# Turning the third group of tokens by transposing transfers, in a fused FFT filter and token-shift MLP kernel

## Chip, core and metric

The kernel runs on one core of a Trainium2 chip. The metric is the device time of one execution in microseconds (us). The core has TensorE (PE, with a separate row PEld for its weight loads), VectorE (DVE), ScalarE (ACT), GpSimd (POOL) and SyncE (SP), whose queue issues every transfer of this kernel.

## The reference

One sequence `x` of 2048 tokens and 448 channels. With `xn` the layer norm of `x` over channels:

```
xn  = layernorm(x)
A   = irfft2(rfft2(xn) * (w_r + i w_i))          # over tokens and channels
h   = gelu(layernorm(xn) @ w1)                   # 448 x 448
hs  = [h0 down 1 | h1 up 1 | h2 down 2 | h3 up 2] @ w2   # quarters of h shifted along tokens
x1  = xn + hs
B   = x1 + gelu(layernorm(x1) @ w3) @ w4         # 448 x 1792, 1792 x 448
out = x + A + B
```

## The kernel before

**Tiles and groups.** The tokens lie in 16 blocks of 128 (token = 16 x partition + block), in four groups of four blocks: group 0 is blocks 14, 15, 0, 1, group 1 is 2 to 5, group 2 is 6 to 9, group 3 is 10 to 13 (`GRP`). A shift along tokens by 1 or 2 is a look at the neighbouring block, so `w2` of a block needs `h` of the blocks at distance 1 and 2.

**Two halves of every number.** Matmuls run in float16. Each operand is split into a high half (ACT rounds to float16) and a low half (DVE or POOL subtracts the high half), and each product is three passes: high by high, high by low, low by high. Weights are first scaled by a power of two that is found from the sum of their squares: ACT squares a piece and accumulates into a column of `m1` to `m4` (`squares`, L243), DVE adds the columns (`pt`, L248), PE adds over the partitions with a matrix of ones (`pm`, L254, in `powers`), DVE makes the scale from the exponent (`pe`, L257 to L260). For w3 this gives `s3`, then eight `w3_split` (ACT L287, DVE L288); for w4 `s4`, then seven `w4_split`.

**The stage around the change, some 10 to 100 us.** For each group:

- `norm1` normalizes the four blocks in place (`xt`).
- Channels are brought to the partitions as `xT`: seven slots of 128 rows, of which the first three and a half hold the high halves and the rest the low ones. Groups 0 to 2 do this with `turn_pe` and `turn_copy`: 16 PE transposes by the identity for a group (L403, tiles `pta`), ACT copies (L413) and DVE subtracts (L414) out of PSUM. Group 3 uses `turn(3)`: ACT and DVE split the normalized block first (L825 to L827), then four transposing transfers, one for a block, write `xT` directly (L828).
- `w1_unit` runs 11 matmuls for a block (L453, tiles `pw1_gi`), a gelu in place (L474), the split into `hs` or a part of `x2mem` (L475, L476), and a transposing transfer into `hT` (L479; called `h0` to `h3` by group, `h30` is group 3's first block).
- `w2_mm`/`w2_tile` runs 12 matmuls for a block (L497, tiles `pw2_b`), DVE adds the result to `xt` (L504).
- `ln2` normalizes blocks again (L525 to L538) and sends them by transposing transfers into `x2all` (L540; tiles `y0`, `y2` and so on).

Behind it comes the MLP by pairs of blocks G = 0 to 7: `front` (L424, tiles `pw3_Gf`, 22 matmuls of 256 columns, gelu L749, split L752 and L753) and `back` (L772). Between the pairs the kernel places the FFT's steps.

**Memory that is shared.** `w1s`, `w2s`, `x2`/`x3` (the split blocks of `turn`), `y` and others take turns in two staging tiles (`stage0`, `stage1`). `w4raw` lies in the same memory `x2mem` as `x2all` from its second quarter on. PSUM banks come in tags of two: `mm`, `tr`, `acc`, `sp`.

**Order.** A scheduler puts the instructions of each engine into one fixed order by its own model; `with behind(key)` says that what stands inside is placed after the instructions kept under that key. That is a placement and not a wait. Each engine then takes its list strictly in order, SP too, so a transfer whose data is not there holds up those behind it. A transposing transfer occupies SP's queue for over a microsecond.

The lines before that are moved:

```
    T1(2)                                   # L922: 16 PE transposes, ACT and DVE copies
    with behind("h", 1, 3):
        load_w3([3])                        # L924: the last 64 rows of w3, loaded twice,
                                            #   into both halves of the partitions (L218)
    for k in range(4):                      # L939: squares of the four tiles of w3
        with behind(*(("a2",), ("a2",), (2, 0), (2, 1))[k]):
            squares(m3[:, k:k + 1], w3raw[:, k])
    with behind("t", 3), behind("h", 2, 3), behind("b0"):
        for i in range(4):                  # L952: w4 in four transfers (L229)
            load_w4(i)
```

Of the kernel before, what the change touches and what calls it, by code (L numbers as in the profile page):

```python
# [13 lines left out]
F16 = mybir.dt.float16  # L14
I32 = mybir.dt.int32
AF = mybir.ActivationFunctionType
ALU = mybir.AluOpType
AX = mybir.AxisListType

S, D, DF, F = 2048, 448, 225, 1792  # L20
# [12 lines left out]
PACE = [(0, 6), (1, 1), (1, 2), (1, 4), (1, 5), (2, 0), (2, 1), (2, 3)]  # L33
FOLD = [(0, 5), (1, 0), (1, 1), (1, 3), (1, 4), (1, 6), (2, 0), (2, 2)]
PIN = [("a3",), ("a3",), ("a3",), ("a3",)]
WMAX = [(1, 4), (1, 5), (1, 6), (2, 0), (2, 1), (2, 2), (2, 3), (2, 4)]
LATE = [(2, 2), (2, 3), (2, 4), (2, 5)]
HS = 3
INV, LAG = 4, 2
# [82 lines left out]
def body(tc, nc, x, wf, w1, w2, w3, w4, c_g, c_n, c_small, out):  # L122
    V, A, P, T, SY = nc.vector, nc.scalar, nc.gpsimd, nc.tensor, nc.sync
# [28 lines left out]
    def bank(tag, name):  # L152
        return ps.tile([128, 512], F32, tag=tag, bufs=2, name=name)
# [17 lines left out]
    def stage(name, n, side, dtype=F32):  # L171
        t = pw.tile([128, 1808], F32, tag=f"stage{side}", bufs=1, name=name)
        return (t if dtype is F32 else t.bitcast(dtype))[:, :n]
# [13 lines left out]
    ones = pc.tile([128, 128], F32, name="ones")  # L187
# [24 lines left out]
    def load_w3(ts):  # L212
        for t in ts:
            if t < 3:
                SY.dma_start(w3raw[:, t], w3[128 * t:128 * t + 128])
            else:
                for h in range(2):
                    SY.dma_start(w3raw[64 * h:64 * h + 64, 3], w3[384:448])  # L218

    load_w3([0, 1])  # L220
    load_x(3)
    load_w3([2])
    x2mem = pw.tile([128, 9 * F], F16, name="x2mem")
    x2all = x2mem[:, 0:8 * F].rearrange("p (j t n) -> p j t n", j=4, t=7)
    w4raw = x2mem.bitcast(F32)[:, F:].rearrange("p (f n) -> p f n", f=14)
# [2 lines left out]
    def load_w4(i):  # L228
        SY.dma_start(w4raw[:, W4F[i]:W4F[i + 1]], w4[:, W4F[i]:W4F[i + 1]])  # L229
# [9 lines left out]
    def squares(col, src, junk=None):  # L239

        n = src.shape[-1]
        junk = xr.bitcast(F16) if junk is None else junk
        return A.activation(out=junk[:src.shape[0], :n], in_=src, func=AF.Square, scale=2.0 ** -20, accum_out=col)  # L243

    def powers(m, n, key, tag="acc", mid=None):

        t = pc.tile([128, 1], F32, name=f"pt{key}")
        i = V.tensor_reduce(out=t, in_=m[:, :n + 1], axis=AX.X, op=ALU.add)  # L248
        after["t" + key] = (i.ins,)
        if mid:  # L250
            with behind("t" + key):
                mid()
        pm = bank(tag, f"pm{key}") if isinstance(tag, str) else tag
        i = T.matmul(pm[:, 0:1], ones, t, start=True, stop=True)  # L254
        after["p" + key] = (i.ins,)
        e = pc.tile([128, 3], I32, name=f"pe{key}")
        V.tensor_scalar(out=e[:, 0:1], in0=pm.bitcast(I32)[:, 0:1], scalar1=1, scalar2=0x7F800000,  # L257
                        op0=ALU.logical_shift_right, op1=ALU.bitwise_and)
        V.tensor_scalar(out=e[:, 1:2], in0=e[:, 0:1], scalar1=-1, scalar2=185 << 23, op0=ALU.mult, op1=ALU.add)
        i = V.tensor_scalar(out=e[:, 2:3], in0=e[:, 0:1], scalar1=1, scalar2=69 << 23, op0=ALU.mult, op1=ALU.add)  # L260
        after["s" + key] = (i.ins,)
        return e.bitcast(F32)[:, 1:2], e.bitcast(F32)[:, 2:3]
# [127 lines left out]
    @contextlib.contextmanager  # L390
    def behind(*key):
        key = key if len(key) > 1 else key[0]
        with contextlib.ExitStack() as st:
            for i in after[key]:
                st.enter_context(tc.issue_after(i))
            yield
# [20 lines left out]
    def T1(g, ts=range(4)):  # L417
        for t in ts:
            turn_copy(g, t, turn_pe(g, t))
# [27 lines left out]
    def w1_in(g, units, ts, passes=range(3)):  # L447
        for p in passes:
            for t in ts:
                for i, pm in units:  # L450
                    wi, xi = ((0, 0), (0, 4), (4, 0))[p]
                    if t < 3 or p != 1:
                        m = T.matmul(pm[:, :D], xTs[g][:, xi + t, 128 * i:128 * i + 128], w1p[:, wi + t],  # L453
                                     start=t == 0 and p == 0, stop=t == 3 and p == 2)
        return m
# [8 lines left out]

    def w1_unit(g, i, pm=None):
        if pm is None:
            pm = bank(("tr" if g == 1 else "mm", "acc")[i // 2], f"pw1_{g}{i}")
            w1_in(g, [(i, pm)], range(4))
        c = CS[GRP[g][i]]
        pm = pm[:, :D]  # L470
        pv_ = pm.rearrange("p (k n) -> p k n", k=4)
        h = hs_buf[c % (HS if g == 3 else HS + 2)]
        with behind(0, i - 2) if g == 0 and i > 1 else contextlib.nullcontext():
            A.activation(out=pm, in_=pm, func=AF.Gelu_apprx_tanh, scale=gsc[:, c:c + 1])  # L474
        u = A.activation(out=h[:, 0, :, 0:112], in_=pv_, func=AF.Copy, scale=h1)  # L475
        v = V.scalar_tensor_tensor(out=h[:, 1, :, 0:112], in0=pv_, scalar=h1, in1=h[:, 0, :, 0:112],  # L476
                                   op0=ALU.mult, op1=ALU.subtract)
        o = h_at(g, i)
        d = SY.dma_start_transpose(out=hT[g][:, :, o:o + 128], in_=h.rearrange("p i k n -> p (i k n)"))  # L479
        after[g, i] = u.ins, v.ins  # L480
        after["h", g, i] = (d.ins,)
# [2 lines left out]

    def w2_mm(b, ks):
        if b not in w2b:
            w2b[b] = bank("sp", f"pw2_{b}")
        for k in ks:
            src, o = b - SHIFT[k], 1
            if src < 0:  # L490
                src, o = src + NB, 0
            elif src >= NB:
                src, o = src - NB, 2
            g, i = WHERE[src]
            o += h_at(g, i) - 1
            for hi, wi in ((0, 0), (0, 1), (1, 0)):
                m = T.matmul(w2b[b][:, :D], hT[g][:112, 4 * hi + k, o:o + 128], w2p[:, wi, k],  # L497
                             start=k == 2 and hi + wi == 0, stop=k == 3 and hi == 1)
        after["w2", b] = (m.ins,)

    def w2_tile(b, ks=(2, 0, 1, 3)):
        w2_mm(b, ks)
        pm = w2b.pop(b)
        V.scalar_tensor_tensor(out=xb(b), in0=xb(b), scalar=cs[:, CS[b]:CS[b] + 1], in1=pm[:, :D],  # L504
                               op0=ALU.mult, op1=ALU.add)
# [313 lines left out]
    def turn(g):  # L819

        xTs[g] = p1.tile([128, 7, 512], F16, tag="xT", bufs=2, name=f"xT{g}")
        y = stage(f"x{g}", 8 * D, 1, F16).rearrange("p (i n) -> p i n", i=4)
        for i, b in enumerate(GRP[g]):
            h, x_ = y[:, i], xb(b)
            u = A.activation(out=h[:, 0:D], in_=x_, func=AF.Copy)  # L825
            V.tensor_tensor(out=h[:, 448:512], in0=x_[:, 384:448], in1=h[:, 384:448], op=ALU.subtract)
            v = V.tensor_tensor(out=h[:, 512:896], in0=x_[:, 0:384], in1=h[:, 0:384], op=ALU.subtract)  # L827
            d = SY.dma_start_transpose(out=xTs[g][:, :, 128 * i:128 * i + 128], in_=h)  # L828
        after["t", g], after[f"a{g}"] = (d.ins,), (u.ins, v.ins)

    def w3_split(i):
        t, cl = i % 4, slice(896 * (i // 4), 896 * (i // 4) + 896)
# [81 lines left out]
            i = P.tensor_tensor(out=w2p[:, 1, k], in0=w2s[:112, k], in1=w2p[:, 0, k], op=ALU.subtract)  # L914
    after["w2p"] = (i.ins,)
    h_alloc(1)
    for k in range(4):
        w1_unit(1, k)
    for b in range(2):
        w2_mm(b, (2, 0))  # L920
    after["T", 2] = after["w2", 1]
    T1(2)  # L922
    with behind("h", 1, 3):
        load_w3([3])  # L924
    with behind("w2p"):
        n1[0][2]()
        n1[1][2]()
        for f in n1[2][:3]:
            f()
    for b in range(2):  # L930
        with behind("T", 2):
            w2_tile(b, (1, 3))
    with behind("a2"):
        n1 = [norm1(3, [P, P, P, P])]
# [1 line left out]
    with behind("w2", 1):  # L936
        for k in range(4):
            w1_unit(2, k)
    for k in range(4):  # L939
        with behind(*(("a2",), ("a2",), (2, 0), (2, 1))[k]):  # L940
            squares(m3[:, k:k + 1], w3raw[:, k])
    s3, r3 = powers(m3, 4, "3", "mm")
    h3 = pc.tile([128, 1], F32, name="h3")
    V.tensor_scalar(out=h3, in0=s3, scalar1=2.0 ** -5, scalar2=None, op0=ALU.mult)
    for b in range(2, 4):
        w2_tile(b)
    turn(3)
    for f in n1[0][:3]:
        f()
    ln2([0, 1], [A, P])  # L950
    with behind("t", 3), behind("h", 2, 3), behind("b0"):
        for i in range(4):  # L952
            load_w4(i)
    for b in range(4, 8):
        w2_tile(b)
        with behind(*PIN[b - 4]):
            w3_split(2 * b - 8)
            w3_split(2 * b - 7)
            for i in (2 * b - 10, 2 * b - 9):
                if i >= 0:  # L960
                    squares(m4[:, i:i + 1], flat(w4raw[:, 2 * i:2 * i + 2]), junk4)
    squares(m4[:, 6:7], flat(w4raw[:, 12:14]), junk4)
    ln2([2, 3], [A, P])
    h_alloc(3)
    for k in range(4):
        w1_unit(3, k)
    with behind("h", 3, 3):
        SY.dma_start(csm, c_small)
    s4, r4 = powers(m4, 7, "4")
    p34 = pc.tile([128, 2], F32, name="p34")  # L970
    V.scalar_tensor_tensor(out=p34[:, 1:2], in0=r3, scalar=2.0 ** 5, in1=r4, op0=ALU.mult, op1=ALU.mult)
# [104 lines left out]
```

## Time and profile before

| | |
|---|---|
| median of 3 runs | 413.37 us (413.05 to 413.66) |
| profiled execution | 413.19 us |
| its span in the profile | 411.4 us |
| mean granted TensorE clock | 0.999 |
| PE busy | 406.0 us, 99% of the span |
| DVE, ACT, POOL busy | 72%, 60%, 28% |
| q1, the queue of all transfers | 43.5% of 16 engines' span |

A row of a timeline is: start and length in us, engine, line, operation, output and inputs, count, and in brackets the idle time before it with what ended it. A row of the groups is: line, engine, operation, names, shapes, count, then busy us and mean ns of one, then idle time before. "DMA to landing" is the time from the start of a transfer's issue to its last byte's arrival. Lines L... are those of the kernel before. PE's matmul rows overlap by about 0.16 us, so the price of one in a row of many is the distance between starts.

### The profile page before, as it was taken

Reading aid. Unit: us, or ns where it says so; the run is one execution under the profiler, and the core shown is the slowest. Engines: PE = TensorE matmul, PEld = TensorE weight load, DVE = VectorE, ACT = ScalarE, POOL = GpSimd, SP = SyncE. Lnnn points to the kernel's source line nnn. Section 1 sums busy time; section 2 is a strip of 40 time slices with the busy share of each in tenths; the row PEclk is TensorE's granted clock in tenths of the full one; section 3 lists DMA queues with packets and bytes.
Section 4 is the critical chain, followed back from the end, with each engine's and each line's share of the span. In section 5 each row is a group of like instructions: output and inputs, shape, how many; then the busy total and the mean of one; then the engine's idle time right before and its main releaser. Section 6 shows DMA issues by size and latency. Waiting matters only on the chain.

```text
span 411.4 us, 8535 instructions
## 1 busy us (share of the span) xinstructions
PE 406.0 (99%) x3314; PEld 290.1 (71%) x3314; DVE 294.4 (72%) x638; ACT 247.7 (60%) x427; POOL 114.6 (28%) x205
## 2 busy tenths in 40 slices
PE   8999999999999999999999999999999999999996
PEld 3655555666667877776887888777776776677885
DVE  5988999897644758863689889875776787667122
ACT  4697979964638766862678888873343434342321
POOL 2987810011217746400031121211212221121000
PEclk9999999999999999999999999999999999999999
DMA  8979499806811383437056655610000213233001
GB/s 279 365 219 202 96 175 324 192 2 142 173 47 45 91 274 132 120 84 165 13 141 178 154 142 143 170 56 2 2 0 2 69 50 107 69 94 130 24 0 46
DMA packets 53496, 48.53 MB, mean 118 GB/s; under 512 B 37600, under 2 KB 48480, under 8 KB 53456
## 3 DMA queue, kind: packets, MB, share of 16 engines
q1 hardware_dynamic: 53456, 47.99, 43.5%
q8 instruction: 26, 0.43, 0.4%
q14 instruction: 14, 0.11, 0.1%
HBM read 35.52 MB, written 3.67 MB: 95 GB/s over the span
## 4 chain that ended last, share of the span: by engine, by line
PE 93%; DVE 3%; DMA 2%; ACT 1%; POOL 1%; issue 0%
PE pw L424 33%; PE acc L772 31%; PE pw L497 8%; PE pw L453 6%; PE pu L693 3%; PE ps L590 3%; PE pp L647 2%; PE pe L713 2%; PE px L664 2%; PE py L735 2%; DMA h<-x2mem 1%; DMA xt<-x 1%; DVE sta L312 1%; PE pta L403 1%; DVE xT L414 0%; DVE xt L352 0%
## 5 line engine op out<-in xcount | busy, mean ns | idle before, releaser
L424 PE MATMUL pw<-x2mem,w3p 128*128 128x256 f16 x1232 | 149.6, 273 | 0.0
L772 PE MATMUL acc<-w4p,hf 128*128 128x448 f16 (+1 forms) x714 | 138.0, 341 | 0.0
L424 PEld LDWEIGHTS <-w3p 128*128 128x128 f16 x1232 | 118.6, 98 | 19.4
L772 PEld LDWEIGHTS <-hf 128*128 128x128 f16 x714 | 69.4, 98 | 48.3 <-DVE hf L753 0.3
L749 ACT ACTIVATE pw<-pw,pe 128x512 f32<-128x512 f32 x56 | 36.7, 656 | 64.6 <-PE pw L424 63.4
L753 DVE SCALAR_TENSOR_TENSOR hf<-pw,h,hf 128x512 f16<-128x512 f32 x56 | 41.9, 749 | 43.6 <-ACT hf L752 43.3
L497 PE MATMUL pw<-w2p,h 112*128 112x448 f16 x192 | 39.4, 352 | 0.1
L752 ACT ACTIVATE hf<-pw,h 128x512 f16<-128x512 f32 x56 | 38.4, 685 | 1.2
L674 POOL TENSOR_TENSOR z<-te 128x450 f32<-128x450 f32 x16 | 16.0, 1003 | 73.0 <-DVE te L672 69.2
L453 PE MATMUL pw<-w1p,xT 128*128 128x448 f16 x176 | 35.1, 352 | 0.3 <-ACT xT L413 0.3
L720 POOL TENSOR_TENSOR e<-e 128x226 f32<-128x226 f32 x16 | 11.5, 721 | 77.8 <-ACT e L717 74.6
L497 PEld LDWEIGHTS <-h 112*128 112x128 f16 x192 | 18.6, 98 | 16.2 <-DMA h<-x2mem 0.5
L453 PEld LDWEIGHTS <-xT 128*128 128x128 f16 x176 | 17.1, 99 | 15.9 <-ACT xT L413 0.5
L654 ACT ACTIVATE pf<-pp 64x450 f16<-64x450 f32 x32 | 17.4, 543 | 16.7 <-DVE pf L655 8.3
L717 ACT ACTIVATE e<-pe 128x452 f32<-128x452 f32 x16 | 8.8, 548 | 26.4 <-PE pe L713 26.4
L655 DVE TENSOR_TENSOR pf<-pp,pf 64x450 f16<-64x450 f32 x32 | 19.9, 622 | 5.9 <-ACT pf L654 5.6
L570 POOL TENSOR_TENSOR xr<-xf 128x452 f32<-128x452 f32 x8 | 8.9, 1115 | 32.0 <-issue 27.6
L669 ACT ACTIVATE te<-px 64x450 f32<-64x450 f32 x32 | 17.3, 539 | 0.5
L728 DVE TENSOR_TENSOR vh<-e,vh 128x448 f16<-128x448 f32 x16 | 10.0, 625 | 9.7 <-ACT vh L727 9.7
L573 POOL TENSOR_TENSOR f<-xr 128x452 f32<-128x452 f32 x16 | 16.1, 1030 | 0.6
L581 DVE TENSOR_TENSOR xh<-f,xh 128x452 f16<-128x452 f32 x16 | 12.7, 833 | 5.0 <-ACT xh L580 5.0
L722 DVE TENSOR_TENSOR e<-e 128x113 f32<-128x113 f32 x16 | 9.9, 618 | 7.8 <-POOL e L720 7.8
(172 smaller groups left out, 600.5 us busy)
## 6 DMA issues: line engine op xcount, KB each, us to landing
wc<-wf SPq DMA_DIRECT2D x32, 225.0 KB, 3.6
wl<-wf SPq DMA_DIRECT2D x8, 450.0 KB, 3.7
xf<-x SPq DMA_DIRECT2D x8, 448.0 KB, 3.4
xt<-x SPq DMA_DIRECT2D x3, 896.0 KB, 11.1
w3raw<-w SPq DMA_DIRECT2D x3, 896.0 KB, 14.6
xr<-x SPq DMA_DIRECT2D x12, 224.0 KB, 2.6
out<-xr SPq DMA_DIRECT2D x12, 224.0 KB, 1.9
gn<-c_g SPq DMA_DIRECT2D x16, 128.0 KB, 3.2
```

The lines of the kernel that those rows point to most:

```text
L424: T.matmul(ps_out, wp[:, wi + t, cols], xT[:, xi + t, tok], start=t == 0 and wi + xi == 0, stop=t == 3 and wi == 4)
L453: m = T.matmul(pm[:, :D], xTs[g][:, xi + t, 128 * i:128 * i + 128], w1p[:, wi + t], start=t == 0 and p == 0, stop=t == 3 and p == 2)
L497: m = T.matmul(w2b[b][:, :D], hT[g][:112, 4 * hi + k, o:o + 128], w2p[:, wi, k], start=k == 2 and hi + wi == 0, stop=k == 3 and hi == 1)
L573: P.tensor_tensor(out=f[:, :, k:k + 2].rearrange("p b s d -> p s b d"), in0=u[:, :, 0], in1=u[:, :, 1], op=op)
L654: A.activation(out=hi, in_=src, func=AF.Copy)
L655: V.tensor_tensor(out=lo, in0=src, in1=hi, op=ALU.subtract)
L669: i = A.activation(out=e[64 * h:64 * h + 64], in_=px_[64 - 64 * h:128 - 64 * h, :2 * DF], func=AF.Copy)
L674: P.tensor_tensor(out=z, in0=t[:, 0], in1=t[:, 1], op=ALU.add)
L749: A.activation(out=pm, in_=pm, func=AF.Gelu_apprx_tanh, scale=r3)
L752: i = A.activation(out=h[:, 0], in_=pm, func=AF.Copy, scale=h3)
L753: j = V.scalar_tensor_tensor(out=h[:, 1], in0=pm, scalar=h3, in1=h[:, 0], op0=ALU.mult, op1=ALU.subtract)
L772: m = T.matmul(to, h[:, hi, o:o + 128], w4p[0][:, wi, f, r], start=f == 0 and n == 0, stop=f == 13 and n == 2)
```

## The change

- Group 2 is turned like group 3: `turn(2)`, four transposing transfers, called behind `w1_unit(1, 0)`, instead of `T1(2)`. Its split blocks lie in `stage0`. The splits of group 1's blocks 2 and 3 are placed behind those of group 2.
- In PE's order the place of the transposes is taken by the first matmuls of `pw2_2` and `pw2_3`, which now use banks of tag `mm`; `pw1_2k` uses `tr` instead of `mm`.
- w3's last 64 rows are loaded once, with the early loads, and copied on chip into the other half of the partitions behind `h20`. Their squares are taken over 64 rows only.
- The product for s3 stands behind `pw1_23`; the eight splits of w3 are placed behind h23's split.
- w4's first two transfers keep their place in the program; the last two, and all seven squares, are placed behind group 3's `h`.
- The maximum of the filter's third piece is placed one step later (`WMAX`).

```diff
-WMAX = [(1, 4), (1, 5), (1, 6), (2, 0), (2, 1), (2, 2), (2, 3), (2, 4)]
+WMAX = [(1, 4), (1, 5), (2, 0), (2, 0), (2, 1), (2, 2), (2, 3), (2, 4)]
...
-                for h in range(2):
-                    SY.dma_start(w3raw[64 * h:64 * h + 64, 3], w3[384:448])
+                SY.dma_start(w3raw[0:64, 3], w3[384:448])
...
-    load_w3([2])
+    load_w3([2, 3])
...
-    def powers(m, n, key, tag="acc", mid=None):
+    def powers(m, n, key, tag="acc", mid=None, pin=None):
...
-        i = T.matmul(pm[:, 0:1], ones, t, start=True, stop=True)
+        with behind(*pin) if pin else contextlib.nullcontext():
+            i = T.matmul(pm[:, 0:1], ones, t, start=True, stop=True)
...
     def w1_unit(g, i, pm=None):
         if pm is None:
-            pm = bank(("tr" if g == 1 else "mm", "acc")[i // 2], f"pw1_{g}{i}")
-            w1_in(g, [(i, pm)], range(4))
+            pm = bank(("tr" if g < 3 else "mm", "acc")[i // 2], f"pw1_{g}{i}")
+            after["u", g, i] = (w1_in(g, [(i, pm)], range(4)).ins,)
...
-        u = A.activation(out=h[:, 0, :, 0:112], in_=pv_, func=AF.Copy, scale=h1)
-        v = V.scalar_tensor_tensor(out=h[:, 1, :, 0:112], in0=pv_, scalar=h1, in1=h[:, 0, :, 0:112],
-                                   op0=ALU.mult, op1=ALU.subtract)
+        with behind("a2") if g == 1 and i > 1 else contextlib.nullcontext():
+            u = A.activation(out=h[:, 0, :, 0:112], in_=pv_, func=AF.Copy, scale=h1)
+            v = V.scalar_tensor_tensor(out=h[:, 1, :, 0:112], in0=pv_, scalar=h1, in1=h[:, 0, :, 0:112],
+                                       op0=ALU.mult, op1=ALU.subtract)
...
-            w2b[b] = bank("sp", f"pw2_{b}")
+            w2b[b] = bank("mm" if b in (2, 3) else "sp", f"pw2_{b}")
...
     def turn(g):
         xTs[g] = p1.tile([128, 7, 512], F16, tag="xT", bufs=2, name=f"xT{g}")
-        y = stage(f"x{g}", 8 * D, 1, F16).rearrange("p (i n) -> p i n", i=4)
+        y = stage(f"x{g}", 8 * D, g - 2, F16).rearrange("p (i n) -> p i n", i=4)
+        done = ()
         for i, b in enumerate(GRP[g]):
             h, x_ = y[:, i], xb(b)
             u = A.activation(out=h[:, 0:D], in_=x_, func=AF.Copy)
             V.tensor_tensor(out=h[:, 448:512], in0=x_[:, 384:448], in1=h[:, 384:448], op=ALU.subtract)
             v = V.tensor_tensor(out=h[:, 512:896], in0=x_[:, 0:384], in1=h[:, 0:384], op=ALU.subtract)
             d = SY.dma_start_transpose(out=xTs[g][:, :, 128 * i:128 * i + 128], in_=h)
-        after["t", g], after[f"a{g}"] = (d.ins,), (u.ins, v.ins)
+            done += (u.ins, v.ins)
+        after["t", g], after[f"a{g}"] = (d.ins,), done
...
     h_alloc(1)
-    for k in range(4):
+    w1_unit(1, 0)
+    turn(2)
+    for k in range(1, 4):
         w1_unit(1, k)
-    for b in range(2):
-        w2_mm(b, (2, 0))
-    after["T", 2] = after["w2", 1]
-    T1(2)
-    with behind("h", 1, 3):
-        load_w3([3])
+    for b, ks in ((0, (2, 0)), (1, (2, 0)), (2, (2, 0)), (3, (2,))):
+        w2_mm(b, ks)
...
-    for b in range(2):
-        with behind("T", 2):
+    with behind("w2", 3):
+        for b in range(2):
             w2_tile(b, (1, 3))
...
+    with behind("h", 2, 0):
+        SY.dma_start(w3raw[64:128, 3], w3raw[0:64, 3])
     for k in range(4):
-        with behind(*(("a2",), ("a2",), (2, 0), (2, 1))[k]):
-            squares(m3[:, k:k + 1], w3raw[:, k])
-    s3, r3 = powers(m3, 4, "3", "mm")
+        n = 128 if k < 3 else 64
+        with behind(*((1, 3), (1, 3), (1, 3), (2, 0))[k]):
+            squares(m3[:n, k:k + 1], w3raw[:n, k])
+    s3, r3 = powers(m3, 4, "3", "sp", pin=("u", 2, 3))
...
-    for b in range(2, 4):
-        w2_tile(b)
+    with behind("p3"):
+        w2_tile(2, (1, 3))
+    w2_tile(3, (0, 1, 3))
     turn(3)
...
     with behind("t", 3), behind("h", 2, 3), behind("b0"):
-        for i in range(4):
+        for i in range(2):
             load_w4(i)
     for b in range(4, 8):
         w2_tile(b)
-        with behind(*PIN[b - 4]):
+        with behind(*PIN[b - 4]), behind(2, 3):
             w3_split(2 * b - 8)
             w3_split(2 * b - 7)
-            for i in (2 * b - 10, 2 * b - 9):
-                if i >= 0:
-                    squares(m4[:, i:i + 1], flat(w4raw[:, 2 * i:2 * i + 2]), junk4)
-    squares(m4[:, 6:7], flat(w4raw[:, 12:14]), junk4)
     ln2([2, 3], [A, P])
     h_alloc(3)
     for k in range(4):
         w1_unit(3, k)
     with behind("h", 3, 3):
+        for i in range(2, 4):
+            load_w4(i)
         SY.dma_start(csm, c_small)
+    for i in range(7):
+        with behind(3, 3):
+            squares(m4[:, i:i + 1], flat(w4raw[:, 2 * i:2 * i + 2]), junk4)
```

## The prediction

> **What bounds the kernel now.** I read the page first. TensorE (PE) is busy for the whole span, and the chain that ended last runs through it:
>
> ```profile
> span 411.4 us, 8535 instructions
> PE 406.0 (99%) x3314; PEld 290.1 (71%) x3314; DVE 294.4 (72%) x638; ACT 247.7 (60%) x427; POOL 114.6 (28%) x205
> ...
> PE 93%; DVE 3%; DMA 2%; ACT 1%; POOL 1%; issue 0%
> ```
>
> The second view was PE's waits. It lists three, together 2 us, all before 12 us, so from there on time is saved by taking work off PE, and lost by any new wait of PE:
>
> ```profile
> PE wps L808 <- DVE wsrc L186: 1.2, 1, 1.2
> PE wps L846 <- DVE xt L352: 0.5, 1, 0.5
> PE pw L453 <- ACT xT L413: 0.3, 1, 0.3
> ```
>
> Third, PE's timeline through the stage that the change rebuilds, 30 to 100 us (start, length, line):
>
> ```profile
> 30.74 2.44 PE L497 MATMUL pw<-w2p,h 112*128 112x448 f16 x12
> 33.01 1.91 PE L403 MATMUL pta<-ident,xt 128*128 128x128 f32 x16
> 34.76 2.68 PE L497 MATMUL pw<-w2p,h 112*128 112x448 f16 x12
> 37.28 8.49 PE L453 MATMUL pw<-w1p,xT 128*128 128x448 f16 x44
> 45.61 6.98 PE L497 MATMUL pw<-w2p,h 112*128 112x448 f16 x36
> 52.42 0.28 PE L254 MATMUL pm<-pt,ones 128*128 128x1 f32 x2
> ...
> 100.19 2.57 PE L424 MATMUL pw<-x2mem,w3p 128*128 128x256 f16 x22
> 102.59 2.43 PE L772 MATMUL acc<-w4p,hf 128*128 128x448 f16 x12
> ```
>
> Rows overlap, so a price is the distance between starts: the 16 transposes of group 2 take 34.76 - 33.01 = 1.75 us; a 448-column matmul (52.42 - 45.61)/36 = 0.189 us; a 256-column one (102.59 - 100.19)/22 = 0.109 us; a `pm` product 0.14 us.
>
> **The change part by part.** *Removed from PE:* the 16 transposes, -1.75 us. In the built order PE is otherwise given the same matmuls: between the end of `pw1_13` and `pw3_04` only their sequence differs, behind that nothing. All the rest is whether PE finds its operands.
>
> *Group 2's copies.* ACT makes four copies of 448 columns instead of four of 512; DVE trades one set of four for another:
>
> ```profile
> 34.28 2.60 DVE L414 TENSOR_TENSOR xT<-pta,xT 128x512 f16<-128x512 f32 x4 [0.46 <-ACT xT L413]
> L827 DVE TENSOR_TENSOR x<-xt,x 128x384 f16<-128x384 f32 x4 | 2.2, 559 | 0.0
> ```
>
> With the small L826 beside it a pair on DVE costs about 0.61 us between starts, 2.45 in all against 2.60: no cost. They no longer wait for PE, which lets DVE work through the three gaps that it has there, 1.2 us:
>
> ```profile
> 31.99 0.68 DVE L476 SCALAR_TENSOR_TENSOR hs<-pw,h,hs 128x448 f16<-128x448 f32 x1 [0.26 <-ACT hs L475]
> 33.14 0.68 DVE L476 SCALAR_TENSOR_TENSOR hs<-pw,h,hs 128x448 f16<-128x448 f32 x1 [0.47 <-ACT hs L475]
> ```
>
> *The four transposing transfers.* SP issues these one behind another. The rows: h11 to h13, the w3 tile behind them, then the landings of `h` (20 to 60 us) and of group 3's own x (L828):
>
> ```profile
> 32.89 4.04 SPq L479 DMA_TRANSPOSE h<-hs  x3
> 36.98 1.22 SPq L218 DMA_DIRECT2D w3raw<-w  x2
> ```
> ```profile
> DMA to landing us min/median/max: 3.0/3.3/4.0
> ```
> ```profile
> DMA to landing us min/median/max: 2.9/3.0/3.1
> ```
>
> One issue takes 4.04/3 = 1.35 us. The built order puts the four between h11 and h12, so they start at 34.25, 35.6, 36.95, 38.3, and the splits are done in time (first at 32.5, last at 34.5). By 3.3 us they land at 37.55, 38.9, 40.25, 41.6. h12 and h13 move from 34.25 and 35.6 to 39.65 and 41.0 and land by 45 at the latest. When does PE ask? In the before trace PE is held once, by h10, on the chain of waits:
>
> ```profile
> 31.53 3.99 DMA h<-x2mem
> ...
> 35.57 1.88 PE pw L497 x9
> ```
>
> h10 is issued as before. PE fills the time ahead of it with nine matmuls of `pw2_2` and `pw2_3` instead of 16 transposes (9 x 0.189 = 1.70), is held until 35.57 again, runs 12 matmuls and asks for the first xT2 at 37.84, for the others at 39.9, 42.0 and 44.1, for h12 and h13 at 46.2. All have landed, the first with 0.3 us to spare; at the 4.0 of the slowest row PE waits 0.4, at 2.9 nothing. I take 0.1.
> The Trainium skill speaks against the exchange: "VectorE: DVE Perf Modes", section "The three transpose paths", gives a 128x128 transpose 390 ns on TensorE and 1309 ns by DMA, and advises TensorE where PSUM will do. The rows bear out neither price here: 109 ns on PE, and 3.0 us for a whole transfer of seven such blocks.
>
> *w3's last tile.* One 64-row load goes out with the early loads, where SP is free; the two of L218 go from SP. The doubling copy on chip has no row. Nearest are those two 64-row loads of the same size, and for who reads it ACT's eight splits of w3:
>
> ```profile
> DMA to landing us min/median/max: 5.1/6.0/6.9
> ```
> ```profile
> 55.68 7.58 ACT L287 ACTIVATE w3p<-w3raw,pe 128x896 f16<-128x896 f32 x8 [0.18 <-DVE pe L259]
> ```
>
> The copy cannot save PE anything, so its bounds are 0 and what 6.9 does. SP issues it behind h20, about 43.7; at 6.9 it lands at 50.6. Its first reader is ACT's fourth split: three of 0.95 behind group 2's last copy, which I count to 49.85, so 52.7. Cost: nothing.
> The skill's "DMA: Bandwidth & Descriptors", section "Anatomy of one DMA", fits 2.0 us plus bytes over 436 GB/s, an estimate of 3.1 us; the sum is the same by it.
>
> *w3's splits earlier.* PE's product for s3 moves ahead of `pw2_2`, from 52.4 to 47, and the eight splits start at about 50 on ACT instead of 55.7. That costs PE nothing, but h30's subtraction now queues behind all eight on DVE.
>
> *w4's second half and its squares.* Issued behind h33; this is the tightest place, so DVE's queue up to h33 must be added up:
>
> ```profile
> 54.25 0.68 DVE L476 SCALAR_TENSOR_TENSOR hs<-pw,h,hs 128x448 f16<-128x448 f32 x1
> ...
> 64.09 2.19 DVE L288 SCALAR_TENSOR_TENSOR w3p<-w3raw,pe,w3p 128x896 f16<-128x896 f32 x2
> ...
> 67.32 0.68 DVE L476 SCALAR_TENSOR_TENSOR hs<-pw,h,hs 128x448 f16<-128x448 f32 x1
> 67.91 0.62 DVE L312 BATCH_NORM_STATS2 stb<-xt 128x6 f32<-128x448 f32 x1
> 68.44 0.67 DVE L504 SCALAR_TENSOR_TENSOR xt<-xt,cs,pw 128x448 f32<-128x448 f32 x1
> 69.03 0.68 DVE L476 SCALAR_TENSOR_TENSOR hs<-pw,h,hs 128x448 f16<-128x448 f32 x1
> ```
>
> Starts give 1.05 us for L288, 0.53 for L312, 0.59 for L504 and L476. Group 2's last subtraction ended at 54.84; the 1.2 us of gaps go, and one L504 and one L312 (1.1) come behind it: 52.4. From there to h33's stand 8 L288, 5 L312, 4 L504, 4 L476 and nine small ones: 8.4 + 2.65 + 2.4 + 2.4 + 0.7 = 16.5, so 68.9. PE's last matmul of `pw1_33` ends at 66.0 (148 of 0.189 and pm3 after 37.84), so DVE sets this. On the way h30 is issued at 64 and lands at 67.3, asked at 69.9; PSUM banks for `pw2_8` come free at 65.7, asked at 68.2.
>
> ```profile
> DMA to landing us min/median/max: 5.7/8.5/10.3
> ```
> ```profile
> 75.96 1.26 SPq L479 DMA_TRANSPOSE h<-hs  x1
> 77.27 0.57 SPq L968 DMA_DIRECT2D csm<-c_small  x1
> ```
> ```profile
> x2mem<-w SPq DMA_DIRECT2D x2, 672.0 KB, 9.7
> ...
> csm<-c_small SPq DMA_DIRECT2D x1, 643.0 KB, 4.8
> ```
> ```profile
> 67.76 0.94 ACT L243 ACTIVATE xr<-x2mem 128x896 f16<-128x896 f32 x1
> ...
> 68.69 0.63 ACT L475 ACTIVATE hs<-pw,h 128x448 f16<-128x448 f32 x1
> ```
>
> h33 goes out from 69.0 to 70.3, the two loads at 70.3 and 70.9 (672 KB each). The nearest row is csm, as large and also right behind h33: 4.8, so 75.1, the second one transfer later, 76.9 (6.0 after its issue). The row of w4's own four loads (the first of these fences: all in flight together) goes to 10.3: 81.2. ACT squares pieces 5 and 6 (0.93 each, a gelu of 0.67 between) and is done at 79.5, DVE's sum at 79.7. PE reaches the s4 product, four matmuls into `pw2_12`, 52 of 0.189 and 47 of 0.109 behind 66.0: 81.0. Cover 1.3 us: no wait by the csm row, 81.2 - 76.9 - 1.3 = 3.0 us by the 10.3 row. I take 0, and 0.2 for all the small covers together (`pw2_13` to `pw2_15` wait for banks that DVE frees 0.7 to 1.0 us ahead).
>
> *The rest:* csm leaves SP earlier, two fold loads go ahead of y8, one maximum of the filter moves by one step; none is asked for before 105 us, and the transfers of y4 still go out behind w4's first splits.
>
> **Sum:** -1.75 + 0.1 + 0.2 = -1.45. The profiled execution took 413.19 (span 411.4 and 1.8 around it), the median of the runs 413.37; I predict on the median: 411.9. Counting the matmuls from 30.74 to 100.19 gives 69.2 of 69.45 us, so no more than 1.75 + 0.25 is to be had: 411.4.
>
> **The rivals.** *DVE becomes the pace* (411.9 becomes 412.9).
>
> ```profile
> 30.00:92.00 62.00, 61.93 (x370) 36.16 (x369) 57.01 (x148) 52.12 (x83) 21.24 (x67) 1.00 0.74 167
> ```
>
> The third busy figure is DVE: 57.0 of 62 us. Its work stays and PE runs 1.75 us shorter, so its 5 us of slack shrink to 3.2. If its queue is 2 us later than added up, banks with covers of 0.7 to 1.0 are late by about 1: 1.45 - 1.0 leaves 412.9. For it: that share. Against: the three gaps above go.
>
> *w4's second half comes too late* (slower). The s4 product stands in PE's queue ahead of five matmuls of `pw2_12` and everything behind, and group 0 of the MLP waits for the scale. It decides when the last load lands after 76.9 + 1.3 = 78.2; beyond 79.7 the gain of 1.45 is gone. At 10.3 us the wait is 3.0: 411.9 + 3.0 = 414.9. Against it: two loads in flight, not four, and the csm row.
>
> *The transfers go block by block.* If each of a transfer's seven 128-wide blocks took the 1.35 us that a whole transfer takes of SP, the fourth would land 4 x 7 x 1.35 = 37.8 us after 34.25, at 72.0, and PE, which asks at 44.1, would lose 28: 440. Every row of L828 (3.1 at most from issue to landing) denies it. The DMA price of the skill's transpose section would do about this.
>
> **Chances.** Forecast (411.3 to 412.5) 0.72; DVE's pace 0.16; late w4 0.11; block by block 0.01. A measurement of this kernel tells some 0.2% (0.8 us) from no change: forecast is faster, the second the same, the last two slower. The range 411.2 to 413.5 takes in the bounds of xT2 (0 to 0.4) and of small covers and most of the second case, and leaves out the last two.
>
> **What would show it.** Right: 32 transposes at L403; `pw1_20` at 37.8 without a wait of over 0.5 us; `pm4` at about 81; the first full 22 of `pw3_04` at 98.4 to 98.8 instead of 100.19, and from there the same distance to the end. Wrong: a wait of PE for DMA xT2, for DVE `pt4` or for DVE L504 between 37 and 95 us; then its length, not the transposes, is the result.

## The result and the profile after

The changed kernel takes 411.51 us (411.13 to 412.15, 6 runs); the kernel before took 413.30 us beside it (413.05 to 414.29, 6 runs). The ratio is 0.9955, 95% interval 0.9942 to 0.9968. A second series of the changed kernel gave 411.81 us (411.20 to 412.50, 7 runs; ratio 0.9965, 0.9954 to 0.9977). The forecast was 411.9, in a range of 411.2 to 413.5, with most of the chance on 411.3 to 412.5. The kernel is faster, as in the case that was held the likeliest.

The profiled execution of the changed kernel took 412.15, the slowest of its six. From its page, and its list of PE's waits (us in total, times, longest):

```profile
span 410.4 us, 8517 instructions
PE 405.0 (99%) x3298; PEld 288.7 (70%) x3298; DVE 294.1 (72%) x642; ACT 247.8 (60%) x427; POOL 116.1 (28%) x205
```

```profile
PE wps L809 <- DVE wsrc L186: 1.2, 1, 1.2
PE pm L254 <- DVE pt L247: 0.6, 1, 0.6
PE pw L453 <- ACT xT L413: 0.3, 1, 0.3
```

PE has 16 instructions less, is 1.0 us less busy and as full as before. One wait is new: `pm` for `pt`, the s4 product. (The half microsecond for `xt` that the list before has at the start is missing here and back in the second profile of this kernel.) PE's timeline (start, length, line) shows where the time went:

```profile
30.63 6.97 PE L498 MATMUL pw<-w2p,h 112*128 112x448 f16 x36
37.44 8.49 PE L453 MATMUL pw<-w1p,xT 128*128 128x448 f16 x44
45.77 0.92 PE L498 MATMUL pw<-w2p,h 112*128 112x448 f16 x4
...
80.05 0.92 PE L498 MATMUL pw<-w2p,h 112*128 112x448 f16 x4
81.58 0.38 PE L254 MATMUL pm<-pt,ones 128*128 128x1 f32 x2 [0.61 <-DVE pt L247]
...
99.25 2.56 PE L424 MATMUL pw<-x2mem,w3p 128*128 128x256 f16 x22
```

From the first w2 product to the full 22 matmuls of `pw3_04` it is 99.25 - 30.63 = 68.62 us, where before had 100.19 - 30.74 = 69.45: 0.83 less, of the 1.75 that left. `pw1_20` starts at 37.44, 6.81 behind the first w2 product, and 36 matmuls of 0.189 are 6.80: the hold of a quarter us that h10 caused before is gone in this profile. The s4 product starts at 81.58, where four matmuls behind 80.05 would have put it at 80.81: 0.77 us lost. From `pw3_04` to the end it is 311.1 us, as before (311.2).

### The profile page after: what moved, and what is told of

It reads as the page before. It is cut to its first block, busy times and chain, and to the rows that moved or that the text cites. A ratio compares the mean times of both kernels' runs of the same rounds, so it can differ in the third digit from the quotient of the medians.

```text
span 410.4 us, 8517 instructions
## 1 busy us (share of the span) xinstructions
PE 405.0 (99%) x3298; PEld 288.7 (70%) x3298; DVE 294.1 (72%) x642; ACT 247.8 (60%) x427; POOL 116.1 (28%) x205
## 4 chain that ended last, share of the span: by engine, by line
PE 84%; DVE 8%; DMA 2%; ACT 2%; issue 2%; SPq 1%; POOL 0%; DVEq 0%; POOLq 0%; ACTq 0%
PE pw L424 32%; PE acc L773 31%; PE pu L694 3%; PE ps L591 3%; PE pp L648 2%; PE pe L714 2%; PE px L665 2%; PE py L736 2%; PE pw L453 2%; PE pw L498 2%; PE wps L809 2%; DVE w3p L288 2%; DMA x2mem<-w 1%; DVE hs L477 1%; DVE xt L505 1%
## 5 line engine op out<-in xcount | busy, mean ns | idle before, releaser
L754 DVE SCALAR_TENSOR_TENSOR hf<-pw,h,hf 128x512 f16<-128x512 f32 x56 | 41.9, 748 | 44.8 <-ACT hf L753 44.5
L498 PEld LDWEIGHTS <-h 112*128 112x128 f16 x192 | 18.7, 98 | 16.5 <-DMA h<-x2mem 0.4
```

Of the source, the lines that this page charges most:

```text
L754: j = V.scalar_tensor_tensor(out=h[:, 1], in0=pm, scalar=h3, in1=h[:, 0], op0=ALU.mult, op1=ALU.subtract)
```

## The experiments

All were run in series beside the kernel before, whose median lay between 413.2 and 413.3 each time. The theory tested is that PE is the pace, so that the 16 transposes taken off it are the gain, and that everything else of the change keeps PE's operands in time. The rivals are named in the expectations.

### The transposes alone, from both sides

**Sixteen dummy transposes** put into PE's queue of the changed kernel:

```
     for b, ks in ((0, (2, 0)), (1, (2, 0)), (2, (2, 0)), (3, (2,))):
         w2_mm(b, ks)
+    for j in range(2):
+        dm = bank("tr", f"dm{j}")
+        with behind("w2", 3):
+            for i in range(8):
+                T.transpose(dm[:, 128 * (i % 4):128 * (i % 4) + 128], ident, ident)
```

> The changed kernel with 16 extra fp32 transposes of the identity put into PE's queue at the place of the old ones, their result unused. Theory (PE is the pace there, and only the wait at the s4 product can swallow extra PE work): +1.75 less up to 0.75, so 412.5 to 413.3. Rival (another engine paces this stage, PE has room): within 0.3 of 411.5.

Measured: 413.74 us (413.43 to 414.25, 11 runs), ratio to before 1.0012 (1.0003 to 1.0021), so 1.9 to 2.2 above the changed kernel: the theory, though 0.4 above the top of its range. Its timeline, and from the list of PE's waits the new one:

```profile
35.44 1.91 PE L930 MATMUL dm<-ident 128*128 128x128 f32 x16
37.19 2.44 PE L498 MATMUL pw<-w2p,h 112*128 112x448 f16 x12
```

```profile
PE pw L498 <- DMA h<-x2mem: 0.5, 1, 0.5
```

The dummies take 37.19 - 35.44 = 1.75 us, the price read off before, and PE has no hole to hide them in. Half a microsecond more goes because the order built around them sends h21 behind group 3's four transfers (issued at 54.11; at 50.01 in the changed kernel). The wait for s4, 0.77 us, is not there in turn, so 0.5 to 0.8 us of the loss stay unaccounted for.

**The transposes back on PE.** Beside the lines shown, the transposes take the PSUM banks `tr` and `acc`, and group 1's splits lose the place that hung on `turn(2)`; all else is as changed:

```
-    turn(2)
...
+    for b in range(2):
+        w2_mm(b, (2, 0))
+    after["T", 2] = after["w2", 1]
+    T1(2)
+    for b, ks in ((2, (2, 0)), (3, (2,))):
+        w2_mm(b, ks)
```

> The changed kernel with one part undone: group 2 is turned by the 16 PE transposes again, everything else (w3's tile, s3's place, late w4) stays. Theory (the gain is the PE time of the transposes): PE gets 1.75 us back; the wait for the s4 product (0.75 us in the profile of the changed kernel) is covered by it in part, so +1.0 to +1.9 on the changed kernel's 411.5, 412.5 to 413.4. Rival (the gain comes from the rearranged w3 and w4 work, the transposes would have hidden): 411.5 plus at most 0.3.

Measured: 414.80 us (414.63 to 415.02, 5 runs), ratio 1.0037 (1.0025 to 1.0050): slower than before, and worse than either theory had it. The list of PE's waits has two beside those of the start:

```profile
PE pw L498 <- DVE xt L505: 0.5, 1, 0.5
PE ps L591 <- DVE xh L582: 0.4, 1, 0.4
```

Between the two profiles (span 413.0 against 410.4) 1.75 us are the transposes and 0.9 these waits; as the wait for s4 is not in it, some 0.7 more must lie in holes too small for the list. So what else the change does is no gain by itself: without the exchange, in this arrangement of banks, it costs 1.5 us against the kernel before.

### The exchange without its company

**The kernel before with the exchange alone.** The run has `turn(2)` and its banks, but w3's last tile in two loads behind h13, w3's splits, w4's loads and its squares as before:

```
-    with behind("h", 2, 0):
-        SY.dma_start(w3raw[64:128, 3], w3raw[0:64, 3])
+    with behind("h", 1, 3):
+        load_w3([3])                       # two 64-row loads
...
-        for i in range(2):
+        for i in range(4):
             load_w4(i)
```

> The kernel before with the exchange of group 2's transposes alone (the copies of turn(2), its transfers behind h11, the shared banks that this frees): w3's last tile comes in two loads behind h13, w3's splits, w4's four loads and w4's squares stand where the kernel before has them. Theory (the exchange is worth its 1.75 us only if h30's transfer does not land behind all of w4, as the run w4_all_early showed): 412.7 to 413.6, with a wait of PE for h30's transfer or for something that hangs on it between 65 and 85 us. Rival (the exchange alone makes the gain, and w4_all_early lost its time because the squares stand late there): 411.4 to 411.9, and no such wait.

Measured: 415.18 us (414.94 to 415.61, 5 runs), ratio 1.0048 (1.0033 to 1.0062). A loss was expected, but not its size, nor its first place. Of the 3.3 us of waits the theory's own, for h30, is the last 0.23. PE's waits and its timeline:

```profile
PE pw L499 <- DMA h<-x2mem: 1.8, 1, 1.8
PE pw L499 <- DMA h<-hs: 1.5, 2, 1.3
```

```profile
46.46 3.57 PE L499 MATMUL pw<-w2p,h 112*128 112x448 f16 x18
51.80 2.44 PE L499 MATMUL pw<-w2p,h 112*128 112x448 f16 x12 [1.77 <-DMA h<-x2mem]
...
63.45 2.44 PE L499 MATMUL pw<-w2p,h 112*128 112x448 f16 x12 [1.29 <-DMA h<-hs]
...
76.06 1.31 PE L499 MATMUL pw<-w2p,h 112*128 112x448 f16 x6 [0.23 <-DMA h<-hs]
```

The queue of SP says why (start, length, line), and below it the landings of what was issued from 44 to 47 us (KB each, median us from issue to landing):

```profile
34.41 5.26 SPq L831 DMA_TRANSPOSE xT<-x  x4
39.77 3.87 SPq L481 DMA_TRANSPOSE h<-hs  x2
43.69 1.22 SPq L218 DMA_DIRECT2D w3raw<-w  x2
45.01 1.26 SPq L481 DMA_TRANSPOSE h<-x2mem  x1
```

```profile
w3raw<-w SPq DMA_DIRECT2D x2, 448.0 KB, 6.0
h<-x2mem SPq DMA_TRANSPOSE x1, 6.7
```

In the kernel before the two w3 loads went out at 36.98, and h20 6.4 us behind them, at 43.34, when nearly all of their bytes were in (their landings are put at about 42 and 44.5); its `h` transfers of 36 to 52 us landed in 3.0 to 3.1. Four transfers more in SP's queue push the w3 loads to 43.69, right ahead of h20, which now lands 6.7 us after its issue, 51.7, and PE waits for it. The wait of 1.29 at 63.45 is for h22, which goes out at 59.13 instead of 54.67 and lands 4.3 us later. This is what the change's w3 half is for: one load that is issued by 11.1 us, and a copy that is issued behind h20.

**All of w4 ahead of h30**, the rest as changed:

```
-        for i in range(2):
+        for i in range(4):
             load_w4(i)
...
-        for i in range(2, 4):
-            load_w4(i)
         SY.dma_start(csm, c_small)
```

> All four loads of w4 are issued ahead of h30, as in the kernel before; the squares stay where the change put them, and everything else of the change stays. Theory (what the change gains is the transposes; the late half of w4 gains nothing by itself, and only brought the late s4 product): 411.1 to 411.7, no wait before the s4 product. Rival (the late half makes room for the transfers of h30 to h32, which land behind 2.5 MB otherwise): h30 lands 2 us later or more, PE waits for it, 412.2 to 413.5.

Measured: 413.41 us (412.88 to 414.04, 11 runs), ratio 1.0004 (0.9995 to 1.0013): the rival. PE's waits, its timeline, and the landing of h30 and h31:

```profile
PE pw L498 <- DMA h<-hs: 1.4, 1, 1.4
```

```profile
70.22 0.54 PE L498 MATMUL pw<-w2p,h 112*128 112x448 f16 x2
72.22 2.63 PE L498 MATMUL pw<-w2p,h 112*128 112x448 f16 x13 [1.45 <-DMA h<-hs]
```

```profile
h<-hs SPq DMA_TRANSPOSE x2, 6.9
```

h30 is issued at 64.97, about a microsecond earlier than in the changed kernel, but all four loads of w4 (3.1 MB) are in flight, and h30 and h31 land 7.2 and 6.6 us after their issues (the row has their median); in the changed kernel the four transfers of h30 to h33 have a median of 3.3. The late half of w4 thus gains nothing of its own: it keeps the road free for h30, at the price of the late s4 product.

**Both halves undone at once**, transposes on PE (the diff of `T1(2)` above) and w4 early (the diff just shown):

> Both halves undone at once: the transposes of group 2 on PE as in the run t1_back, and all four loads of w4 ahead of h30 as in w4_all_early; w3's last tile, its earlier splits and the place of w4's squares stay as changed. With these three the four corners are known: transfers and late half 411.5 to 411.8, transfers and early 413.4, PE and late 414.8. Theory (the early loads cost time only where PE asks for h30 soon; with 1.75 us of transposes on PE it asks later, and the kernel before had all four early without a wait): 413.0 to 413.6, as the kernel before, and faster than PE and late. Rival (the two add up): 414.8 + 1.7 = 416.5.

Measured: 415.27 us (415.15 to 415.75, 5 runs), ratio 1.0051 (1.0038 to 1.0064). The theory fell: it is not the kernel before again. The two losses do not add up to 416.5 either; beside the kernel with PE's transposes and the late half (414.80) the early loads cost 0.5. What still differs from before are the places of w4's squares, of w3's splits and of the banks; the list of waits has 0.7 for `xt` L505 and 0.3 for h30. Which of them makes the 2.0 us was not taken apart, and no run takes the step of the filter's maximum (`WMAX`) alone.

**w3's last tile by two loads at the start**, no doubling copy; every compute engine's order stays:

```
                 SY.dma_start(w3raw[0:64, 3], w3[384:448])
+                SY.dma_start(w3raw[64:128, 3], w3[384:448])
...
-    with behind("h", 2, 0):
-        SY.dma_start(w3raw[64:128, 3], w3raw[0:64, 3])
```

> w3's last tile comes by two 64-row loads from HBM in the first 20 us instead of one load and a doubling copy on chip; every engine's own order is that of the changed kernel. Theory (the copy is done long before its first reader and SP has room for it, so it neither costs nor gains): 411.4 to 411.9. Rival (the copy's 298 GB/s at 44 to 46 us slow xT2 and h12, h13, or its issue delays xT3): 411.0 or less; or the second load of 448 KB delays the start: 412.2 or more, with the first w2 matmul behind 31.2.

Measured: 413.06 us (412.58 to 414.91, 12 runs), ratio 1.0002 (0.9992 to 1.0012): the second rival, and 1.25 to 1.55 us above the changed kernel. The profiled execution is the slowest of the twelve (414.91), so its wait is longer than the usual one. PE's waits and timeline, SP's queue, and the landing of h00:

```profile
PE pw L499 <- POOL w2p L918: 1.5, 1, 1.5
```

```profile
32.51 7.49 PE L499 MATMUL pw<-w2p,h 112*128 112x448 f16 x36 [1.49 <-POOL w2p L918]
```

```profile
26.08 6.10 SPq L481 DMA_TRANSPOSE h<-hs  x3
```

```profile
h<-hs SPq DMA_TRANSPOSE x1, 6.4
```

h00 is issued at 26.08 while the loads of the start still run, and lands 6.4 us later, at 32.5; in the changed kernel it landed in 3.6, and the three issues took 4.10 us instead of 6.10. The list names POOL as the releaser, whose `w2p` of the other two quarters ends at that moment; but in the changed kernel the same instructions end at 32.3 and PE's first w2 product, of quarters 2 and 0, starts at 30.63 without them. With 448 KB more the last starting load lands at 30.9 instead of 27.9, and that is enough to put h00 behind them.

### The covers of the new transfers

**xT2 later.** `turn(2)` stands behind all four `w1_unit(1, k)`, and nothing of group 1 waits for its copies:

```
     w1_unit(1, 0)
-    turn(2)
     for k in range(1, 4):
         w1_unit(1, k)
+    turn(2)
...
-        with behind("a2") if g == 1 and i > 1 else contextlib.nullcontext():
+        with contextlib.nullcontext():
```

> Group 2's four copies and transfers stand behind group 1's first products in the source, so that SP issues them between h11 and behind h13, not all four behind h11. Theory (the first transfer has 0.3 us to spare, the fourth little more): PE waits for DMA xT2 at pw1_20 or in its fourth step, 1 to 2.5 us in all, 412.3 to 413.8. Rival (the order has more room than counted; what else PE has to do fills the time): 411.8 or less, and no wait for xT2 in the list.

Measured: 413.38 us (412.73 to 414.46, 11 runs), ratio 1.0006 (0.9998 to 1.0015): the theory by its time; the wait for xT2 is smaller than it said (1 to 2.5 us) and comes at the third block. From PE's waits:

```profile
PE pw L453 <- DMA xT<-x: 0.6, 1, 0.6
PE pw L498 <- DVE xt L505: 0.5, 1, 0.5
```

With the four transfers spread from 34.67 to 43.98 PE waits 0.6 us for the third, at `pw1_22`; another half us is a bank that DVE frees late at 82 us. Putting all four ahead of h12 and h13 matters, though the two waits do not add up to the 1.6 to 1.9 us above the changed kernel.

### The late s4 product

**A place of its own for x2.** In the changed kernel group 2's split blocks lie in `stage0`, which y0 takes next:

```
-        y = stage(f"x{g}", 8 * D, g - 2, F16).rearrange("p (i n) -> p i n", i=4)
+        y = x2mem[:, 4096:4096 + 8 * D] if g == 2 else stage(f"x{g}", 8 * D, g - 2, F16)
+        y = y.rearrange("p (i n) -> p i n", i=4)
```

> The changed kernel with group 2's split blocks in a stretch of x2mem of their own instead of the staging tile that y0 takes next; the order on every engine is the same. Theory (y0 waits in the profile until the fourth xT2 transfer has landed, 43.5 us, and that delays group 3's normalization, DVE, h30, h33, w4's last load and so the s4 product by about 1.3 us): the wait of PE at the s4 product goes from 0.75 to 0, 410.8. Rival (w4's last load is late by its own transfer, not by what stands ahead): PE still waits 0.6 or more, 411.5.

> The run own_stage once more, as its time did not show the 0.4 to 0.7 us that its profile gained between the first w2 matmul and pw3_04. Theory (the gain is real, but below what few executions tell): median 411.2 to 411.6. Rival (the gain is lost at another place): 411.7 to 411.9 again, and the profile shows the wait for the s4 product under 0.2 us and as much lost before 31 us or behind 99 us.

Measured: 411.82 us (411.29 to 412.14, 5 runs), ratio 0.9964 (0.9951 to 0.9976), and again 411.49 us (411.35 to 412.11, 5 runs), ratio 0.9959 (0.9947 to 0.9971). The wait went as the theory had it, the time of 410.8 did not come. How the wait arises is told by the changed kernel's rows of POOL and SP:

```profile
43.75 0.64 POOL L528 TENSOR_SCALAR y<-xt,nm 128x448 f32<-128x448 f32 x1 [2.20 <-ACT xr L242]
44.38 3.62 POOL L352 TENSOR_SCALAR xt<-xt,vy,nma 128x448 f32<-128x448 f32 x4
```

```profile
65.92 6.06 SPq L480 DMA_TRANSPOSE h<-hs  x4
72.03 1.05 SPq L228 DMA_DIRECT2D x2mem<-w  x2
```

POOL stands 2.2 us ahead of y0, which may not overwrite x2 before the fourth transfer has read it, landed at about 43.5 (the row's "ACT xr" had long ended). Group 3's normalization is behind that, and through DVE the chain to h30 and h33. In the profiles with a place of its own the same POOL instruction starts at 41.84 and 41.77 without a wait, and for the s4 product PE's timeline shows (second profile):

```profile
80.21 0.92 PE L498 MATMUL pw<-w2p,h 112*128 112x448 f16 x4
81.00 0.38 PE L254 MATMUL pm<-pt,ones 128*128 128x1 f32 x2
```

81.00 is 0.03 behind the 80.97 at which the four matmuls end: no wait, and from the first w2 product (30.74) to `pw3_04` (98.62) 67.88 us. The first profile has a wait of 0.18, too short for the list, and 67.96 us.

Two things keep this from showing that the place is the cure. In both profiles the fourth transfer also landed sooner, 3.1 us after its issue instead of 5.3, at 41.7 and 41.6, so that y0 need not have waited in `stage0` either. In the run with the late half ahead of h33 (below) x2 does lie in `stage0`, the transfer landed at 42.0, and y0 waited 0.23 us. What made the wait is the late landing, and the cause of that is open. The other thing is that DVE's queue gained a microsecond (h30's subtraction starts at 64.22 instead of 65.18) and h33's subtraction only 0.3: it now waits for ACT. The rows are ACT's in the changed kernel and DVE's in the first profile of this run:

```profile
69.37 0.63 ACT L476 ACTIVATE hs<-pw,h 128x448 f16<-128x448 f32 x1 [2.96 <-DMA h<-hs]
```

```profile
69.72 0.68 DVE L477 SCALAR_TENSOR_TENSOR hs<-pw,h,hs 128x448 f16<-128x448 f32 x1 [0.60 <-ACT hs L476]
```

Group 3 has three `hs` buffers, so h33 takes the one that h30's transfer reads, and ACT may write it only when that has landed: 69.26 in the changed kernel and 68.94 here, where h30, issued 1.0 us earlier, took 4.0 us to land instead of 3.3.

**The late half ahead of h33**, and **both cures together**:

```
-    with behind("h", 3, 3):
+    with behind("h", 3, 2):
         for i in range(2, 4):
             load_w4(i)
+    with behind("h", 3, 3):
         SY.dma_start(csm, c_small)
```

> The changed kernel with w4's third transfer ahead of h33's transfer instead of behind it; the scheduler also puts the s4 product four matmuls earlier in PE's queue. Theory (the s4 product waits for the last load): the last load lands about 1 us earlier, the product is asked for 0.75 earlier; PE's wait goes from 0.75 to about 0.5, 411.2 to 411.4. Rival (the transfers share the same time whatever their order, h33 is late instead): wait of 1.5 or more at the s4 product or at h33's matmuls, 412.2.

> Both cures of the late s4 product together: group 2's split blocks in a place of their own, and w4's second half issued ahead of h33. Theory (run to run the wait is small, each cure alone is as good as both): 411.2 to 411.8, no wait of PE before the s4 product. Rival (each cure gains 0.5 us and loses it by its own effect elsewhere): 412 or more, with a new wait of PE before 100 us that the trace names.

Measured: 411.86 us (411.52 to 412.44, 5 runs) and 411.80 us (411.61 to 412.40, 5 runs), ratios 0.9965 (0.9952 to 0.9979) and 0.9968 (0.9955 to 0.9980). Neither profile has the wait; the same distance is 67.88 and 67.83 us. The first theory (411.2 to 411.4) is missed in time, the second (411.2 to 411.8) is met at its upper end.

**The changed kernel once more:**

> The changed kernel once more, unaltered, beside the variants of this call. Theory: the 0.8 us that PE stood before the s4 product belongs to the one profiled execution, the slowest of its six; another profile shows it between 0 and 0.8, with the fourth 448-column part of pw2_12 to pm4 1.1 to 1.9 us apart, and the start of the first w2 matmul moves by up to 0.3 us from profile to profile. Time 411.3 to 411.8. Rival: the wait is in every execution of this order; then it is 0.7 to 0.8 again, and the two earlier variants without it owed their equal time to something lost elsewhere.

Measured: 411.81 us (411.20 to 412.50, 7 runs), with the wait in its profile too:

```profile
PE pm L254 <- DVE pt L247: 0.5, 1, 0.5
```

It is 81.62 against 80.16 + 0.76, so 0.7 by PE's rows, as the rival has it, and the fourth xT2 transfer is late again (5.1 us). But both profiled executions are slow ones of their series (412.15, the slowest of six, and 412.16, the second slowest of seven), and whether the faster executions have the wait no run shows. The cures take it away in the profile, 0.4 to 0.8 us by PE's rows, and the medians do not show it: 411.49 to 411.86 for the cures, 411.51 and 411.81 for the changed kernel. Series of one and the same kernel differ by 0.3 us, and the first w2 product starts anywhere from 30.63 to 31.16 in these profiles; a gain of more than half a microsecond would have been seen. Where the rest goes is open, and no version here is shown to beat the changed kernel.

## Why the prediction was right

**The 1.75 us.** Right: PE is the pace, 16 transposes take 1.75 us, and the dummy run loses them again in full, and more.

**xT2.** Right, 0.1 us taken and nothing lost: `pw1_20` came at 37.44, without the hold for h10 that the prediction kept (37.84). That is no gain of the change: in five other profiles with the same order up to there the hold is 0.1 to 0.3 us. The four landed in 3.0, 3.1, 3.0 and 5.3 us, SP's issues took 1.31 each (1.35 taken). That the fourth could land outside 2.9 to 4.0 was not foreseen; it landed at 43.49, and PE asked at 43.68 (37.44 and 33 matmuls), so 0.2 us was all that was left. The Trainium skill's rule ("VectorE: DVE Perf Modes", section "Rules for kernel authors") to transpose 128x128 on TensorE where a result in PSUM will do would have refused the change, which gained 1.4 to 1.8 us. Taken alone, though, the exchange loses 1.9 us (415.18), by the rows for the order and load of SP's queue and not for the price of a transpose.

**w3's doubling copy.** Right that it costs nothing here: it landed in 4.4 us, at 48.95, below the bound of 6.9 and long ahead of its reader. The estimate of 3.1 us from the Trainium skill's "DMA: Bandwidth & Descriptors" (section "Anatomy of one DMA — SWDGE (gpsimd) path") is too low for it; that fit is for transfers issued from GpSimd, and this one goes from SP. But "cannot save PE anything" holds only against the kernel before. Against a second load at the start it saves 1.25 us or more, and the place behind h13 that the kernel before had was seen to hold up h20 in the run with the exchange alone. The prediction priced each edit against the order before; it did not ask what the exchange would cost if the w3 loads stayed, which is what ties the parts together.

**w4's second half.** This is the step with the error. The landings were well placed: 4.5 and 6.1 us after the issue, against 4.8 and 6.0. The issue was not: 72.03 instead of 70.3, because h33's subtraction came at 70.03 to 70.71 instead of ending at 68.9. Two terms were missed, and in this profile they end together. DVE's queue was added up rightly (16.5 us from the end of h23's subtraction to that of h33's) but begins 1.8 us late, at 54.2 instead of 52.4. About 1.0 of this is POOL, which waits for the fourth transfer of xT2 because x2 lies where y0 goes; the rest is not taken apart. And "DVE sets this" left out ACT, whose rounding of h33 waits until h30's transfer has landed, and ends at 70.00. So even with DVE a microsecond earlier h33 gained 0.3. Of the cover of 1.3 us nothing was left and PE waited 0.77. That is the "too late" rival in a small dose; the sum had allowed 0.2 for all such covers. It is also the sign of being wrong that the prediction named, a wait for DVE `pt4`; it is the smaller part of the result here, not the larger.

**DVE as the pace.** Not seen in the changed kernel: no wait for a bank in the list. Five of the variants have such a wait, of 0.2 to 0.7 us in all for `xt` L505 (L506 in one).

**Sum.** -1.75 for the transposes, about -0.25 for h10, +0.77 for s4 and some 0.4 in small pieces make the -0.83 of the profile. `pw3_04` came at 99.25, outside the 98.4 to 98.8 that the prediction gave as a sign of being right. The profiled execution is the slowest of its six, so this is the low end: the medians of the two series are 1.4 and 1.8 us below before's, and the forecast was 1.45 below before's median. The main term is shown by the runs; that the total comes so close is in part luck, as h10's hold and the s4 product were both off, in opposite ways.

## What to carry to other kernels

Where one engine is the pace, an instruction removed from it pays its own time only if every operand behind it can come that much earlier; look for the transfer that becomes the next late one, and for a buffer that comes free only when a transfer has landed, as `hs` here. In these runs a transposing transfer behind 0.9 to 3.1 MB of plain loads landed some 3 to 4 us later, so place bulk loads where no one waits for the next transpose, and when SP gets more to issue, count what the push does to every load behind. A change of several parts is judged whole: here each of three parts, left out or put elsewhere, cost the whole gain or nearly so.

## What the runs showed of the hardware

Transposing transfers that landed in 3.1 to 3.6 us in the changed kernel (h00, h20 and h30) took 6.4, 6.7 and 7.2 us in runs with more plain loads in flight ahead of them (the last of the starting loads, two of 448 KB, four of w4), on the same queue of SP. They held up the queue as well: with all of w4 ahead the issue of h31, right behind h30, took 4.63 us, against 1.27 in the changed kernel.

Three transposing transfers in a row of the changed kernel's profile, the fourth xT2 and h12 and h13, took 5.3, 4.9 and 4.5 us with no plain load beside them. From 41.75 to 43.25 us, while they were due, all transfers of the core together moved 0.01 MB. Why is not shown.
